# Two unused 96-byte tiles behind the right-hand weight pools of a fused linear-attention and two-MLP kernel

## The chip, the cores and the metric

The kernel runs on one core of one Trainium2 chip. The metric is the device time of one execution in microseconds (us): the median over several runs. The profile is one execution, taken by the hardware profiler; its span is the time from the first to the last instruction. Engines are named as in the profile: PE (TensorE matmul), PEld (TensorE weight load), DVE (VectorE), ACT (ScalarE), POOL (GpSimd), SP (SyncE, which issues most DMAs).

## The reference

Three stages follow each other, in float32.

```python
# 1. delta-rule linear attention: B=4, H=8, S=768, D=48
k_n = k / (norm(k) + 1e-6)
for t in range(S):
    y[t] = q[t] @ state
    v_old = state^T k_n[t]
    state = state + beta[t] * outer(k_n[t], v[t] - v_old)
# 2. squared-relu MLP on x = y as [3072 tokens, 384]
x = relu(x @ w_in) ** 2 @ w_out          # 384 -> 2048 -> 384
# 3. max-of-three MLP
h = maximum(maximum(x @ w1, x @ w2), x @ w3)   # 384 -> 768
out = h @ w_out2                                # 768 -> 384
```

## The kernel before

**Stages.** The 768 positions are cut into six steps of 128 positions; with four batches a step holds 512 tokens. Per step the attention runs in chunked form (`gram`, `solve`, `values`, `chain`: thousands of small float32 matmuls of 32 to 64 columns, long chains of small DVE operations in `solve`). `moe1` then does the first MLP for the 512 tokens of the step: 16 blocks of 128 hidden features, per block nine matmuls into one bank (`hidden`) and nine into three accumulating banks (`project`). After the last step comes the second MLP: `maxout` (27 matmuls per block of 128 features, six blocks) and `project2` (18 matmuls per 128 tokens). The small attention matmuls of later steps are interleaved with `moe1` of earlier ones; from about 515 us on no attention is left.

**Wide matmuls.** Every float32 operand of the two MLPs is kept as two float32r parts, high and low (names ending in h and l), and a product is made of three matmuls (`three`: high by high, high by low, low by high). One matmul has a stationary operand of 128x128, which PE loads first (a weight load, PEld), and a moving operand of 512 columns, which it streams. In `moe1` the stationary tiles are `wih`, `wil` (first weights) and `wo` (a ring of four, second weights), the moving ones are `xh`, `xl` and `gh`, `gl`. In `maxout` the stationary tiles are `b0h` to `b2l` and the moving ones `xh`, `xl` or `x2h`, `x2l`. In `project2` the stationary tiles are the hidden values `m0h`, `m0l` or, in turn by step, `m1h`, `m1l`, and the moving ones are the weights `b3h`, `b3l` with 384 columns.

**Order.** A planner in the kernel records all operations of stage one and two, and of stage three apart, and writes out a fixed order on each engine by its own costs and due times. Each engine then works through its order strictly. Every operation is issued by one helper, so all rows of the profile have line L330, and they are told apart by tile names.

**Places in memory.** Tiles lie in pools of SBUF. The left pools (`const`, the attention pool `apool`, later `bwp`) grow from low addresses, the right ones from the top of the memory downwards: `wpool` holds `wih`, `wil` and the four `wo`; after it is closed, `bsb` holds `m1h` and `m1l`. Within a partition all left tiles that wide matmuls read (`xh`, `xl`, `gh`, `gl`, `x2h`, `x2l`, all `b` tiles, `m0h`, `m0l`) start at byte 384 of a 512-byte block, since the tiles ahead of them come to such a sum and each of them is a multiple of 512 bytes. All tiles of the two right pools are multiples of 512 bytes too and start at byte 480 of a block, 96 bytes further. A stationary slice of 128 float32 values is 512 bytes long, a moving one 2048 (or 1536 in `project2`), so all slices keep the offset of their tile.

Of the kernel before, what the change touches and what calls it, by code (L numbers as in the profile page):

```python
# [10 lines left out]
F32 = mybir.dt.float32  # L11
# [324 lines left out]
def kernel(  # L336
# [31 lines left out]
    P = 128  # L368
# [29 lines left out]
    wpool = es_w.enter_context(tc.tile_pool(name="wpool", bufs=1, side="right"))  # L398
# [13 lines left out]
    def tiles(pool, n, shape, dtype, name):  # L412
        return [pool.tile(shape, dtype, tag=f"{name}{i}", name=f"{name}{i}") for i in range(n)]

    def one(pool, shape, dtype, name):
        return pool.tile(shape, dtype, tag=name, name=name)
# [20 lines left out]
    wih = one(wpool, [P, KD, DFF], F32R, "wih")  # L437
    wil = one(wpool, [P, KD, DFF], F32R, "wil")
    wo_ring = Ring(tiles(wpool, 4, [P, 2, DM], F32R, "wo"))

    kq = [one(apool, [P, 2, HP, 2, 64], F32, x) for x in ("kt", "qt")]
    kt, qt = ([x[:, i] for i in range(2)] for x in kq)
# [492 lines left out]
    with tc.manual_schedule():  # L935
# [71 lines left out]
        def load_x2(t):  # L1007
            raw, (hi, lo) = x2r[t % len(x2r)], x2()
            pl.sync.dma_start(out=raw, in_=x2d[t].rearrange("r p c -> p r c"))
            for r in range(KD):  # L1010
                pl.scalar.activation(hi[:, r], raw[:, r], AF.Copy)
                pl.vector.tensor_tensor(lo[:, r], raw[:, r], hi[:, r].bitcast(F32), op=sub)
            return hi, lo

        def maxout(f, x, m2):
            ph = []
            fs = slice(f * P, f * P + P)
            for i in range(3):
                ph.append(b_ring())
                for r in range(KD):  # L1020
                    with pl.together():
                        three(ph[i], bw[i, "h"][:, r, fs], bw[i, "l"][:, r, fs],
                              x[0][:, r], x[1][:, r], r == 0, r == KD - 1)
                    pl.at += 1
            m = r_ring()
            pl.scalar.activation(m, ph[0], AF.Copy)
            pl.vector.tensor_tensor(m, m, ph[1], op=ALU.max)
            pl.vector.tensor_tensor(m, m, ph[2], op=ALU.max)
            pl.scalar.activation(m2[0][:, f], m, AF.Copy)
            pl.vector.tensor_tensor(m2[1][:, f], m, m2[0][:, f].bitcast(F32), op=sub)  # L1030

        def project2(t, b, m2):
            po = o_ring()[:, 0:DM]
            bs = slice(b * P, b * P + P)
            for f in range(NF2):
                with pl.together():
                    three(po, m2[0][:, f, bs], m2[1][:, f, bs], bw[3, "h"][:, f],
                          bw[3, "l"][:, f], f == 0, f == NF2 - 1)
                pl.at += 0.75
            ob = ob_ring()  # L1040
            pl.scalar.activation(ob, po, AF.Copy)
            pl.sync.dma_start(out=ov[t, b], in_=ob)
# [9 lines left out]
        es_w.close()  # L1052
        bsb = ctx.enter_context(tc.tile_pool(name="bsb", bufs=1, side="right"))
        m_all.append([one(bsb, [P, NF2, TB], F32R, "m1" + x) for x in "hl"])
        for n, t in enumerate(order):
            if n + 1 < NS:
                x = x2() if order[n + 1] == NS - 1 else load_x2(order[n + 1])
                maxout(0, x, m_all[(n + 1) % 2])
            for b in range(B):
                project2(t, b, m_all[n % 2])  # L1060
            if n + 1 < NS:
                for f in range(1, NF2):
                    maxout(f, x, m_all[(n + 1) % 2])
# [31 lines left out]
```

## Time and profile before

| | |
|---|---|
| median of 3 runs | 951.26 us (950.89 to 952.01) |
| span of the profiled execution | 946.6 us |
| median less that span | 4.7 us |
| PE busy | 879.0 us, 93% of the span |
| PEld busy | 733.6 us, 77% |
| DVE busy | 588.9 us, 62% |
| ACT busy | 443.7 us, 47% |
| PE matmuls | 9388 |

The profile gives no time for the profiled execution other than its span, so the 4.7 us stand for what lies before the first and after the last instruction and for the difference between executions. Ends of matmuls are modelled: how close together matmuls run is read from the distance between their starts, not from their durations (a 512-column matmul shows some 390 to 406 ns and the next one starts long before that).

### The profile page before, as it was taken

The numbers are of one execution on the slowest core, as the hardware profiler recorded it, in microseconds if no ns is written. First come the engines' busy times: TensorE is split into PE (matmuls) and PEld (weight loads), VectorE is DVE, ScalarE is ACT, GpSimd is POOL, SyncE is SP. The second block draws the span as 40 slices with busy tenths as digits, with TensorE's granted clock in tenths as the row PEclk, the third lists the DMA queues.
The fourth block names the chain that finished last, engine by engine and source line by source line (L and its number), as shares of the span: only waits on it lengthen the run. The fifth ranks groups of instructions, "written<-read, shape, count | busy, mean of one in ns | idle before, by whom it ended". The sixth has DMA issues, their size and how long they took to land.

```text
span 946.6 us, 22413 instructions
## 1 busy us (share of the span) xinstructions
PE 879.0 (93%) x9388; PEld 733.6 (77%) x9388; DVE 588.9 (62%) x1256; ACT 443.7 (47%) x835; POOL 23.3 (2%) x33
## 2 busy tenths in 40 slices
PE   5536789999999989999999999999999999999998
PEld 4426778877777777877887888888898989898987
DVE  4999998899758957955953499893323232323221
ACT  6446468974465464565456567663222122121121
POOL 2001001000000010010000000000000000000000
PEclk9555799999999999999999999999999999999999
DMA  9744468777646646343422567670020100000000
GB/s 169 145 117 124 105 186 228 164 179 181 155 97 123 171 93 117 112 119 79 125 85 86 184 189 230 185 224 6 1 68 1 68 1 34 0 26 9 26 9 34
DMA packets 186276, 100.64 MB, mean 106 GB/s; under 512 B 150080, under 2 KB 166208, under 8 KB 186176
## 3 DMA queue, kind: packets, MB, share of 16 engines
q1 hardware_dynamic: 185328, 99.02, 40.3%
q8 instruction: 73, 1.20, 0.5%
q10 hardware_dynamic: 848, 0.20, 0.1%
q14 instruction: 27, 0.22, 0.1%
HBM read 79.53 MB, written 14.94 MB: 100 GB/s over the span
## 4 chain that ended last, share of the span: by engine, by line
PE 78%; DVE 14%; ACT 4%; issue 2%; DMA 1%; DVEq 0%; ACTq 0%
PE ps L330 78%; DVE xs L330 3%; DVE T L330 2%; DVE tmp L330 2%; DVE t L330 2%; ACT G L330 1%; DVE W L330 1%; DMA raw<-in_moe_w_in_dram 1%; DVE L L330 1%; ACT W L330 1%; ACT r L330 1%; DVE wil L330 1%; ACT US L330 1%; DVE gl L330 0%; DVE US L330 0%
## 5 line engine op out<-in xcount | busy, mean ns | idle before, releaser
L330 DVE TENSOR_TENSOR r<-r,ps 128x512 f32<-128x512 f32 x72 | 49.5, 688 | 178.7 <-PE ps L330 176.7
L330 PE MATMUL ps<-gh,wo 128*128 128x512 f32 (+1 forms) x624 | 159.5, 384 | 1.1 <-ACT gh L330 0.9
L330 ACT ACTIVATE r<-ps 128x512 f32<-128x512 f32 (+1 forms) x140 | 80.0, 572 | 165.3 <-PE ps L330 149.2
L330 PEld LDWEIGHTS ps<-gh,wo 128*128 128x128 f32 x624 | 111.6, 190 | 26.1 <-ACT gh L330 1.4
L330 PE MATMUL ps<-xh,wih 128*128 128x512 f32 (+1 forms) x312 | 123.1, 395 | 2.0 <-ACT r L330 1.7
L330 PE MATMUL ps<-xh,wil 128*128 128x512 f32 (+1 forms) x312 | 119.3, 382 | 0.9 <-issue 0.9
L330 PE MATMUL ps<-xl,wih 128*128 128x512 f32 (+1 forms) x312 | 119.0, 381 | 0.0
L330 DVE TENSOR_TENSOR gl<-r,gh 128x512 fp32r<-128x512 f32 (+1 forms) x104 | 67.1, 647 | 52.9 <-ACT gh L330 50.5
L330 PE MATMUL ps<-gl,wo 128*128 128x512 f32 (+1 forms) x312 | 85.9, 383 | 2.5 <-DVE gl L330 1.3
L330 PEld LDWEIGHTS ps<-xh,wih 128*128 128x128 f32 x312 | 59.7, 191 | 16.3 <-ACT r L330 3.5
L330 PEld LDWEIGHTS ps<-xh,wil 128*128 128x128 f32 x312 | 60.0, 192 | 12.3 <-issue 1.3
L330 PEld LDWEIGHTS ps<-xl,wih 128*128 128x128 f32 x312 | 59.8, 192 | 11.9
L330 PEld LDWEIGHTS ps<-gl,wo 128*128 128x128 f32 x312 | 56.4, 190 | 15.3 <-DVE gl L330 1.9
L330 ACT ACTIVATE gh<-r 128x512 fp32r<-128x512 f32 (+1 forms) x104 | 62.0, 596 | 10.0 <-PE ps L330 7.6
L330 ACT ACTIVATE G<-ps 32x256 f32<-32x256 f32 (+3 forms) x132 | 55.4, 432 | 22.5 <-PE ps L330 20.4
L330 DVE TENSOR_TENSOR T<-T,tmp 128x31 f32<-128x31 f32 (+15 forms) x186 | 63.0, 338 | 3.5
L330 DVE TENSOR_TENSOR tmp<-L,T 128x31 f32<-128x31 f32 (+15 forms) x186 | 62.8, 337 | 3.3
L330 ACT ACTIVATE r<-r 128x512 f32<-128x512 f32 (+1 forms) x104 | 62.0, 596 | 2.4
L330 PE MATMUL ps<-W 64*64 64x64 f32 x1536 | 47.0, 249 | 12.3 <-ACT W L330 9.7
L330 PEld LDWEIGHTS ps<-W 64*64 64x64 f32 x1536 | 40.2, 159 | 19.2 <-ACT W L330 12.2
L330 DVE TENSOR_SCALAR xs<-xs 128x384 f32<-128x384 f32 x112 | 40.6, 362 | 16.4 <-ACT xs L330 15.6
L330 ACT ACTIVATE m0h<-r 128x512 fp32r<-128x512 f32 x18 | 11.4, 632 | 67.2 <-DVE r L330 67.2
(149 smaller groups left out, 1663.0 us busy)
## 6 DMA issues: line engine op xcount, KB each, us to landing
wo<-wod SPq DMA_DIRECT2D x88, 384.0 KB, 3.4
raw<-in_moe_w_out_dram SPq DMA_DIRECT2D x22, 384.0 KB, 3.6
raw<-in_moe_w_dram SPq DMA_DIRECT2D x18, 384.0 KB, 3.9
raw<-in_moe_w_in_dram SPq DMA_DIRECT2D x16, 384.0 KB, 4.2
wod<-wo SPq DMA_DIRECT2D x16, 384.0 KB, 3.7
vn<-in_v_dram SPq DMA_DIRECT2D x24, 192.0 KB, 4.3
kn<-in_k_dram SPq DMA_DIRECT2D x24, 192.0 KB, 4.4
out_dram<-ob SPq DMA_DIRECT2D x24, 192.0 KB, 1.9
```

Source lines behind the costliest of these rows:

```text
L330: self.plan.add(self.name, lambda: fn(*args, **kw), cost, [out], ins, flow, late)
```

## The change

Two tiles that nothing writes or reads are allocated, one as the last tile of `wpool`, one as the last of `bsb`, each of 24 float32 values (96 bytes) per partition. As the right-hand pools end at the top of the memory, each pool starts 96 bytes lower: `wih`, `wil`, `wo` and `m1h`, `m1l` then start at byte 384 of a 512-byte block in place of 480. Nothing else has another address. The order of instructions is the same as before on all five engines, and so are the semaphores that each waits for.

```diff
@@ -437,6 +437,7 @@
     wih = one(wpool, [P, KD, DFF], F32R, "wih")
     wil = one(wpool, [P, KD, DFF], F32R, "wil")
     wo_ring = Ring(tiles(wpool, 4, [P, 2, DM], F32R, "wo"))
+    one(wpool, [P, 24], F32, "edge")
@@ -1052,6 +1053,7 @@
         es_w.close()
         bsb = ctx.enter_context(tc.tile_pool(name="bsb", bufs=1, side="right"))
         m_all.append([one(bsb, [P, NF2, TB], F32R, "m1" + x) for x in "hl"])
+        one(bsb, [P, 24], F32, "edge1")
```

## Rows read from the trace of the kernel before

**Rows 1.** Busy time of each engine in three stretches of the span.

```profile
core 0: us, PE busy (x) PEld busy (x) DVE busy (x) ACT busy (x) POOL busy (x), PEclk, DMA share, GB/s
0.00:226.00 226.00, 172.66 (x2839) 146.96 (x2840) 204.16 (x515) 137.54 (x293) 12.90 (x22) 0.83 0.65 159
226.00:435.00 209.00, 198.31 (x3376) 158.71 (x3374) 153.18 (x302) 115.09 (x205) 8.55 (x9) 1.00 0.54 123
435.00:645.00 210.00, 210.00 (x1766) 168.91 (x1767) 147.30 (x317) 126.17 (x227) 1.89 (x2) 1.00 0.52 155
```

**Rows 2.** Chain of work that ended last, its longest piece: start, us, what.

```profile
434.97 508.01 PE ps L330 x3072
```

**Rows 3.** Timeline of PE in the first MLP: start us, us, matmul.

```profile
599.69 0.40 PE L330 MATMUL ps<-xh,wil 128*128 128x512 f32 x1
...
602.97 0.40 PE L330 MATMUL ps<-xh,wih 128*128 128x512 f32 x1
```

**Rows 4.** Timeline of PE in maxout of the second MLP.

```profile
685.16 0.39 PE L330 MATMUL ps<-xl,b0h 128*128 128x512 f32 x1
...
690.15 0.33 PE L330 MATMUL ps<-b3h,m0h 128*128 128x384 f32 x1
```

**Rows 5.** Busy time by engine, first MLP, with much and little beside it.

```profile
550.00:640.00 90.00, 90.00 (x386) 72.34 (x385) 79.11 (x169) 61.92 (x114) 0.00 (x0) 1.00 0.67 209
...
640.00:644.50 4.50, 4.50 (x21) 3.62 (x20) 0.69 (x1) 2.14 (x4) 0.00 (x0) 1.00 0.02 4
```

**Rows 6.** Timeline of PE at the seam of the two MLPs.

```profile
646.29 0.39 PE L330 MATMUL ps<-x2l,b0h 128*128 128x512 f32 x1
...
647.20 0.62 PE L330 MATMUL ps<-gh,wo 128*128 128x512 f32 x2
...
653.43 0.39 PE L330 MATMUL ps<-x2h,b1h 128*128 128x512 f32 x1
...
655.47 0.39 PE L330 MATMUL ps<-x2h,b0h 128*128 128x512 f32 x1
```

**Rows 7.** Timeline of PE where maxout follows project2.

```profile
702.65 0.39 PE L330 MATMUL ps<-xh,b0h 128*128 128x512 f32 x1
...
704.74 0.39 PE L330 MATMUL ps<-xh,b1h 128*128 128x512 f32 x1
```

**Rows 8.** Busy time by engine in project2, first with m1, then with m0.

```profile
740.00:751.00 11.00, 11.00 (x65) 11.00 (x64) 1.00 (x2) 2.10 (x4) 0.00 (x0) 1.00 0.15 54
...
789.00:800.00 11.00, 11.00 (x65) 11.00 (x65) 1.25 (x2) 2.11 (x4) 0.00 (x0) 1.00 0.13 47
```

**Rows 9.** Groups of PE, 226 to 435 us: count, busy us, mean ns.

```profile
L330 PE MATMUL ps<-gh,wo 128*128 128x512 f32 x202 | 55.5, 401 | 0.0
L330 PE MATMUL ps<-xh,wih 128*128 128x512 f32 x96 | 39.5, 411 | 0.4 <-ACT r L330 0.4
```

**Rows 10.** Groups of PE by form, 435 to 653 us.

```profile
L330 PE MATMUL ps<-gh,wo 128*128 128x512 f32 x276 | 73.6, 398 | 0.0
L330 PE MATMUL ps<-xh,wih 128*128 128x512 f32 x132 | 53.0, 402 | 0.0
```

**Rows 11.** Timeline of PE: matmuls of 256 columns; later, small ones in a row.

```profile
153.12 0.87 PE L330 MATMUL ps<-gh,wo 128*128 128x256 f32 x6
...
155.94 0.51 PE L330 MATMUL ps<-gl,wo 128*128 128x256 f32 x3
...
176.81 1.16 PE L330 MATMUL ps<-W 64*64 64x64 f32 x64
```

**Rows 12.** Groups by form: DVE's writes of low weight parts, right and left.

```profile
L330 DVE TENSOR_TENSOR wil<-xs,wih 128x384 fp32r<-128x384 f32 x16 | 8.8, 552 | 2.9 <-ACT wih L330 2.8
...
L330 DVE TENSOR_TENSOR b1l<-xs,b1h 128x384 fp32r<-128x384 f32 x6 | 3.3, 557 | 0.8 <-ACT b1h L330 0.6
```

**Rows 13.** DMA issues into a right-hand tile: count, size, us to landing.

```profile
wo<-wod SPq DMA_DIRECT2D x88, 384.0 KB, 3.4
```

## The prediction

> **What bounds the kernel now.** I read the busy time by stretches first. Up to 226 us DVE works 204 of 226 us and PE waits for it; from 226 to 435 us PE works 198.3 of 209 us; from 435 us on it has no idle time at all (210.00 of 210), at a granted clock of 1.00, which is the 2.4 GHz level [rows 1]. The chain that ended last says the same: its last 508 us are PE alone, 3072 matmuls without a break [rows 2]. So from 435 us to the end each nanosecond between two matmuls counts in full, before 226 us hardly any does, and in between it is mixed.
>
> Then the pace of the wide matmuls, by their starts in the timeline, where no attention is left. In the first MLP 14 matmuls of 512 columns take 602.97 - 599.69 = 3.28 us, 234.3 ns each [rows 3]. In the second MLP 22 matmuls of the same size take 690.15 - 685.16 = 4.99 us, 226.8 ns each [rows 4]. At 2.4 GHz 512 columns are 213.3 ns, so the one kind has 21 ns on top and the other 13.5. Both have the same shapes, moving tiles from the left pools (`xh` and `xl` in both) and a new weight load for each matmul. What differs: the stationary tile of the first lies in the right pool, 96 bytes off the moving tile within 512, that of the second in the left pool, at the same offset.
>
> Other differences have to be ruled out. The first MLP has DVE, ACT and DMAs beside it, the second little. But with DVE busy 79 of 90 us and DMA at 0.67 the 90 us hold 386 matmuls (two of them cut by the edges: 234.4 ns each), and in 4.5 us with DMA at 0.02, hardly any DVE and the same tiles there are 21 (again two cut: 234 to 237 ns) [rows 5]. The activity beside it doesn't set the pace. At the seam the two kinds stand mixed within 10 us: the last four of a left-hand group take 0.91 us, 228 ns each; then 27 matmuls, of which 9 are right-hand ones in groups of two or three, take 6.23 us, 231 ns each, left-hand ones among them too; then nine left-hand ones 2.04 us, 226.7 ns each [rows 6]. A right-hand load disturbs, and those behind it need some matmuls to find back.
>
> **The change, part by part.**
>
> *First pool (`wih`, `wil`, `wo`).* Nothing is added to any engine and nothing is moved in any order; the wide matmuls of the first MLP get the offsets of those in the second. If the offset is what differs, each gains 234.3 - 226.8 = 7.5 ns.
>
> From 435 us to the end of the first MLP there are 276 with `gh` and `wo`, half as many, 138, with `gl`, and three times 132 with `wih` and `wil` [rows 10], 810 in all: 810 x 7.5 = 6.1 us. Not each runs at the best pace at once: behind `project2`, where the width changes, the first nine left-hand matmuls take 2.09 us, 232.2 ns each, 49 ns more in all than nine at 226.8 [rows 7]. Each cluster of small attention matmuls will cost such a restart. Between 435 and 645 us there are 1766 matmuls less some 780 wide ones [rows 1, 10], about 985 small ones; a cluster is some 64 of them [rows 11], so about 15 restarts, 0.75 us. That leaves 5.3 us, on the path in full (PE never waits there).
>
> From 226 to 435 us there are 202 + 101 + 3 x 96 = 591 [rows 9], 4.4 us. Some 2785 small matmuls [rows 1] make about 44 restarts, 2.2 us. Of the 2.2 us left I take half, 1.1 us: PE idles 10.7 us of this stretch, and where it waits for a result of ACT or DVE, a faster PE only waits longer. The bounds are 0 and 4.4.
>
> Before 226 us I take nothing: what hides it is DVE's 204 of 226 us [rows 1]. The 256-column matmuls stand there, 24 of them in 155.94 - 153.12 = 2.82 us, 117.5 ns each [rows 11], 10.8 over their columns. With the 13.5 of the left-hand ones they would be slower, by 2.7 ns; there are 288 (the first `HALF` = 8 blocks of the first step, done in two halves of the tokens: 2 x 8 x 18), 0.8 us at most if the cover were gone.
>
> *Second pool (`m1h`, `m1l`).* I take nothing. Here the trace has both cases side by side: 11 us of `project2` hold 65 matmuls of 384 columns with the right-hand `m1` and 65 with the left-hand `m0` [rows 8]. This row is also the best argument against the whole theory, since the same 96 bytes do no harm there; the offset then must matter for 512 columns and not for 384. As the weights in rows 3 and 4 differ by place alone, and clearly, I keep to it, but not with certainty.
>
> *Others that touch the tiles.* DVE writes a low part of 384 columns in 552 ns to the right and 557 to the left [rows 12]: nothing. The DMAs into `wo` land after 3.4 us [rows 13] and no stretch from 435 us on shows PE idle for them; even some tenths more would be hidden by the ring of four.
>
> *Sum.* 5.3 + 1.1 = 6.4 us: a span of 946.6 - 6.4 = 940.2 us, and from the median 951.26 (4.7 us above that span) 944.9 us. Its own range: without any restart loss and with all of the middle stretch 6.1 + 4.4 = 10.5 us, 940.8; with twice the restart loss and nothing from the middle 6.1 - 1.5 = 4.6 us, 946.7. What is late next: nothing from 435 us on, since ACT has 126 and DVE 147 busy of 210 us there; at a pace 3% faster DVE goes from 79 to about 82 of each 90 us in its fullest part [rows 5].
>
> **The rivals.**
>
> *Nothing changes (951.3 us).* The offset isn't the cause, but something that goes with the right pool or with the first MLP, such as the distance in memory or the change between two kinds of moving tile; then the change moves addresses and no time. For it: rows 8, equal for both pools. Against it: the seam [rows 6], where the pace follows the stationary tile, and the best pace survives the change of `x2h`, `x2l` and of the `b` tiles.
> The Trainium skill speaks for this rival: "TensorE: Matmul & The Clock Gate", section "Step-by-step: what each phase is for", says that PE has two independent read ports to SBUF, and that loading the next weights takes no read bandwidth from the running matmul. By that rule no placement matters and the time stays. The trace agrees in rows 8 and not in rows 3 against rows 4.
>
> *A small part only (949.0 us).* The good pace is reached but not kept: the first MLP goes between two kinds of moving tile and two of weights every nine matmuls, and if each such change is a restart, all run at the 232.2 ns of rows 7, 2.1 ns better than now: 810 x 2.1 = 1.7 us and half of 591 x 2.1 = 0.6, together 2.3 us. For it: the second MLP never shows such alternation. Against it: there the changes of tile go by unseen.
>
> *Slower (959.6 us).* Two reads at one offset meet each other and hinder each other more than two 96 bytes apart, in the first MLP, where a load follows each matmul. The price, for want of a row, is the same difference with its sign turned: 7.5 ns x (810 + half of 591) = 8.3 us. It decides from 1.7 ns per wide matmul on (1.9 us over 1105). Against it: the left-hand tiles have equal offsets and run best.
>
> **How the numbers follow.** My forecast 0.71, the small part 0.11, nothing 0.12, slower 0.06. About 0.2%, 1.9 us, is what a measurement of this kernel can tell from no change; forecast and small part lie beyond it, so faster is 0.82, same 0.12, slower 0.06. The predicted time is the forecast's, 944.9 us. The range takes in its own bounds and the small part, 940.8 to 949.0, and leaves out 0.18.
>
> **What would show it.** In the profile after, the starts in the first MLP without attention should lie 227 ns apart in place of 234.3, and a window of 90 us there should hold some 397 matmuls in place of 386; the second MLP should be unchanged, `project2` at 65 in 11 us for both; the first MLP's last matmul should come 5 to 7 us earlier, with PE still without idle time from 435 us on; the stretch before 226 us should keep its length. The prediction is wrong if the pace stays at 234 (the pool or the stage, not the offset), settles at about 232 (restarts), or rises. It is wrong in its size if the middle stretch gives all or none, which PE's idle time between 226 and 435 us would show.

## The result and the profile after

The changed kernel takes 942.44 us (median of 6 runs, 939.6 to 943.68) against 951.24 us before (6 runs): ratio 0.9904, 95% interval 0.9887 to 0.9921, so 7.5 to 10.7 us faster. The profiled execution has a span of 940.6 us, 6.0 us less than before, and took 943.03 us as a whole, one of the longer of the six. The six executions of the changed kernel take 2.1 to 3.1 us more than their spans; by that the kernel before, with a span of 946.6 us, took about 949 us when it was profiled (an estimate), less than each of its six timed runs (950.53 to 953.11). So the two profiles show less of the gain than the medians do.

Busy time of each engine after, in the stretches of [rows 1]:

```profile
0.00:226.00 226.00, 169.53 (x2836) 144.27 (x2837) 204.20 (x513) 137.50 (x293) 12.90 (x22) 0.83 0.65 158
226.00:435.00 209.00, 196.88 (x3394) 159.72 (x3396) 153.30 (x304) 114.97 (x205) 8.56 (x9) 0.99 0.55 124
435.00:645.00 210.00, 210.00 (x1788) 173.04 (x1781) 147.46 (x319) 126.46 (x228) 1.90 (x2) 1.00 0.51 155
```

The first two stretches look much as before (2836 and 3394 matmuls against 2839 and 3376), DVE still fills the first one, and PE still never idles in the third, but holds 22 matmuls more there. The end of the chain that ended last, after (start, us, what), shows the same by time:

```profile
434.14 0.56 issue
434.70 502.30 PE ps L330 x3071
937.07 0.49 ACT ob L330
```

The long piece of PE begins at the same place as before, 434.70 against 434.97 us, and takes 502.30 us in place of 508.01 [rows 2]. So 5.7 of the 6.0 us come behind 435 us and 0.3 us ahead of it.

The timeline of PE after, first MLP, at the place of [rows 3], then the seam of the two MLPs, at the place of [rows 6]:

```profile
599.33 0.39 PE L330 MATMUL ps<-xh,wil 128*128 128x512 f32 x1
...
600.46 1.52 PE L330 MATMUL ps<-gh,wo 128*128 128x512 f32 x6
601.82 0.84 PE L330 MATMUL ps<-gl,wo 128*128 128x512 f32 x3
602.50 0.39 PE L330 MATMUL ps<-xh,wih 128*128 128x512 f32 x1
```

```profile
641.26 0.62 PE L330 MATMUL ps<-gh,wo 128*128 128x512 f32 x2
...
645.34 0.39 PE L330 MATMUL ps<-x2h,b2h 128*128 128x512 f32 x1
```

From 599.33 to 602.50 us there are 14 matmuls in 3.17 us, 226.4 ns each, where there were 234.3. At the seam 18 matmuls that go between right-hand and left-hand weights seven times take 4.08 us, 226.7 ns each: the disturbance is gone, and a change of tile is no restart. Ninety microseconds of the first MLP, and 11 us each of `project2`, first with `m1`, then with `m0`, answer to [rows 5] and [rows 8]:

```profile
550.00:640.00 90.00, 90.00 (x399) 74.53 (x398) 77.97 (x167) 61.56 (x114) 0.00 (x0) 1.00 0.64 202
735.00:746.00 11.00, 11.00 (x65) 11.00 (x64) 0.65 (x1) 1.48 (x3) 0.00 (x0) 1.00 0.16 56
784.00:795.00 11.00, 11.00 (x66) 11.00 (x65) 0.69 (x1) 1.66 (x4) 0.00 (x0) 1.00 0.15 54
```

399 matmuls in place of 386, and `project2` as it was.

### The profile page after: what moved, and what is told of

Same layout as the page of the kernel before. It is cut to its first block, busy times and chain, and to the rows that moved or that the text cites. A ratio compares the mean times of both kernels' runs of the same rounds, so it can differ in the third digit from the quotient of the medians.

```text
span 940.6 us, 22413 instructions
## 1 busy us (share of the span) xinstructions
PE 868.4 (92%) x9388; PEld 731.2 (78%) x9388; DVE 588.4 (63%) x1256; ACT 443.1 (47%) x835; POOL 23.4 (2%) x33
## 4 chain that ended last, share of the span: by engine, by line
PE 74%; DVE 14%; ACT 5%; DMA 3%; issue 3%; SPq 0%; DVEq 0%; ACTq 0%
PE ps L330 74%; DVE xs L330 3%; DVE T L330 2%; DVE tmp L330 2%; ACT G L330 2%; DVE t L330 2%; DVE W L330 1%; DMA raw<-in_moe_w_out_dram 1%; DMA raw<-in_moe_w_in_dram 1%; ACT r L330 1%; ACT W L330 1%; DVE gl L330 1%; ACT US L330 1%; DVE L L330 1%; ACT xs L330 0%
## 5 line engine op out<-in xcount | busy, mean ns | idle before, releaser
L330 PE MATMUL ps<-gh,wo 128*128 128x512 f32 (+1 forms) x624 | 156.3, 379 | 2.8 <-ACT gh L330 2.0
```

Source lines behind the costliest of these rows:

```text
L330: self.plan.add(self.name, lambda: fn(*args, **kw), cost, [out], ins, flow, late)
```

## The experiments

"Distance" below is the start of the stationary tile less that of the moving tile, within 512 bytes: 96 before, 0 in the changed kernel, in the first MLP. The left pools could be shifted too, by a tile ahead of `ident` or as the first of `bwp`. A pace is the mean time between the starts of neighbouring wide matmuls, from the 20th of an unbroken row of them on, read from the trace of each kernel (steps of over 300 ns, where PE waited, are left out). All distances tried are multiples of 32 bytes.

**One pool at a time.**

```diff
     # e1_first_pool
+    one(wpool, [P, 24], F32, "edge")
     # e2_second_pool
+        one(bsb, [P, 24], F32, "edge1")
```

> Only the tile behind the first pool (wih, wil, wo); m1 stays 96 bytes off. If the whole gain comes from the 512-column matmuls of the first MLP, this kernel does all that the change does: about 942 us, first MLP at 227 ns per wide matmul, 6 us less span from 435 us on. If m1 has a share, it lies between 942 and 951 us, and project2 with m1 shows it.

> Only the tile behind the second pool (m1h, m1l); the first pool stays 96 bytes off. If the offset matters for 512 columns and not for the 384 of project2: no change, 951 us, first MLP at 234 ns. If m1 has a share: below 950 us, and project2 with m1 would have more than 65 matmuls in 11 us.

The first pool alone gives 940.68 us against 950.09 on that chip, ratio 0.9908 (0.9884 to 0.9932), with the first MLP at 227 ns. The second alone gives 949.21 us, ratio 0.9995 (0.9979 to 1.0012), with the first MLP at 234 ns. The last pieces of their chains, e1 and then e2, where the kernel before has 508.01 us [rows 2]:

```profile
433.99 502.27 PE ps L330 x3072
```

```profile
434.39 508.10 PE ps L330 x3072
```

The whole effect is that of `wih`, `wil` and `wo`; the second unused tile does nothing that these runs can tell.

**Equal distance or good alignment.**

```diff
     # e3_left_moved
+    one(const, [P, 24], F32, "edge0")
     ident = one(const, [P, P], F32, "ident")
     # e4_right_at_128
+    one(wpool, [P, 88], F32, "edge")
+        one(bsb, [P, 88], F32, "edge1")
```

> All left tiles move 96 bytes up to offset 480, the right ones stay at 480: offsets are equal again, but no tile lies on a 64-byte boundary. Theory 'equal offset of stationary and moving tile': both MLPs at 227 ns per wide matmul, about 942 us. Theory 'alignment' (a tile at 480 is badly placed, one at 384 well): both MLPs at 234 ns, some 7 us more in the second MLP than before, about 958 us.

> Right tiles moved 352 bytes down, to offset 128: on a 128-byte boundary, but 256 bytes from the left ones within 512. Theory 'alignment': 227 ns per wide matmul, about 942 us. Theory 'equal offset': the first MLP is not at 227 ns; if any difference disturbs alike, 234 ns and 951 us; project2 with m1, 256 bytes off now, shows whether 384 columns stay free of it at that distance as well.

Windows of the first MLP, of e3 and then of e4 (80 us long; the kernel with a distance of -96, below, has 344 there):

```profile
550.00:630.00 80.00, 80.00 (x355) 66.24 (x354) 73.55 (x159) 56.43 (x105) 0.00 (x0) 1.00 0.67 208
```

```profile
550.00:630.00 80.00, 80.00 (x355) 66.24 (x354) 72.94 (x158) 55.70 (x104) 0.00 (x0) 1.00 0.68 208
```

Both have the good pace. e3, with every tile off the 64-byte boundaries, still runs both MLPs at 227 ns: alignment is not the cause. But e4 runs at 227 ns as well with a distance of 256, and 941.7 us, ratio 0.992 (0.9895 to 0.9945), is as good as the changed kernel: equal offsets are not needed. Each theory lost one of the two tests. e3 as a whole gained less, 944.04 us, ratio 0.9948 (0.9929 to 0.9966); its last piece of PE is as short (502.32 us) but begins at 436.91 us, so what it loses lies ahead of that, and why was not found.

**A table of distances.** Six kernels, each with a tile in `wpool`, which sets the distance of the first MLP, and one at the start of `bwp`, which sets that of `maxout` with `xh` (with `x2h` it stays 0).

```diff
     # e5, e6, e7, e8: n = 8, 120, 16, 48 and m = 8, 40, 48, 24;  e11, e12: n = 72, 56 and m = 56, 72
+    one(wpool, [P, n], F32, "edge")
         bwp = ctx.enter_context(tc.tile_pool(name="bwp", bufs=1))
+        one(bwp, [P, m], F32, "edge2")
```

> Right tiles 64 bytes past the left ones (offset 448), and the second MLP's left tiles 32 bytes past xh and xl, so that maxout with xh has a distance of 32 and with x2h one of 0. 'Any multiple of 64 is good': first MLP 227 ns, maxout with xh 234 ns. 'Any multiple of 128' or 'of 256': both 234 ns. 'Only a short way past the moving tile is bad': both 234 ns. Maxout with x2h 227 ns by all.

> Right tiles 128 bytes past the left ones (offset 0), the second MLP's left tiles 160 past xh. 'Multiple of 64' and 'of 128': first MLP 227 ns, maxout with xh 234 ns. 'Multiple of 256': both 234 ns. 'Only a short way past is bad' (32 to 96 bytes): both 227 ns.

> Right tiles 32 bytes past the left ones (offset 416), the second MLP's left tiles 192 past xh. 'Multiple of 64': first MLP 234 ns, maxout with xh 227 ns. 'Multiple of 128' or '256': both 234 ns. 'Only a short way past is bad': first MLP 234 ns, maxout with xh 227 ns.

> Right tiles 96 bytes short of the left ones (offset 288), the second MLP's left tiles 96 past xh: the distance of the kernel before, now within the left pool and in the second MLP. If the distance is the cause, maxout with xh runs at 234 ns (486 matmuls, 3.6 us more in the second MLP) and with x2h at 227; if pool or stage is, at 227 both. First MLP: 'multiple of 64, 128 or 256' 234 ns, 'only a short way past is bad' 227 ns.

e8 answers whether pool or stage has a part: `maxout` of the second MLP, all tiles left, in the timeline of PE, first with `x2h` (distance 0), then with `xh` (distance 96):

```profile
656.16 0.39 PE L330 MATMUL ps<-x2h,b0h 128*128 128x512 f32 x1
...
660.92 0.39 PE L330 MATMUL ps<-x2h,b2h 128*128 128x512 f32 x1
```

```profile
700.87 0.39 PE L330 MATMUL ps<-xh,b1h 128*128 128x512 f32 x1
...
705.79 0.39 PE L330 MATMUL ps<-xh,b0h 128*128 128x512 f32 x1
```

Each pair of rows spans 21 matmuls: 4.76 us, 226.7 ns each, and 4.92 us, 234.3 ns each. That is to the tenth the pace of the first MLP before. The same weights, in the same pool and stage, lose 7.6 ns per matmul by a distance of 96 alone; that it isn't `xh` itself, the kernel before shows, where the same tiles at a distance of 0 take 226.8 ns [rows 4]. The window of its first MLP (distance -96, that is 416):

```profile
550.00:630.00 80.00, 80.00 (x344) 64.35 (x344) 71.74 (x154) 54.45 (x101) 0.00 (x0) 1.00 0.64 203
```

As 32, 64, 128, 160, 192 and 416 all disturb, neither a multiple of 64 or 128 nor "a short way past" fits; 256 was the only multiple left that did. The last two kernels of this kind looked for a still better place:

> Right tiles 320 bytes past the left ones, the second MLP's left tiles 224 past xh. 'Only multiples of 256 hold the best pace': both 229 to 234 ns. 'The disturbance shrinks towards 256' (192 gave 228.9): 224 at 227 to 229, 320 alike.

> Right tiles 384 bytes past the left ones, the second MLP's left tiles 288 past xh. 'Only multiples of 256': both 229 to 234 ns. 'Shrinks towards 256, grows beyond': 288 near 227 to 229, 384 near 233. A pace below 226.7 at any distance would make a kernel faster than the changed one.

The paces found, in ns, 512 columns (with the kernel that gave each), and the same for `project2` with 384 columns, whose distance is that of `m1` and `b3`:

```
distance   512 columns                           384 columns (project2, m1)
  0        226.7  after, e1, e3                  173.3  after, e3, e8
 32        233.3  e5 (maxout), e7
 64        233.3  e5                             175.4  e5
 96        234.3  before; e8 (maxout)            173.3  before, e1
128        232.6  e6
160        233.3  e6 (maxout)
192        228.9  e7 (maxout)
224        233.3  e11 (maxout)
256        226.8  e4                             173.3  e4
288        233.3  e12 (maxout)
320        233.3  e11                            175.4  e12
384        232.5  e12                            176.1  e11
416        233.4  e8                             176.7  e7
448                                              173.3  e6
```

Of the distances tried, only 0 and 256 keep the best pace for 512 columns, and the four pairs that lie 256 apart (32 and 288, 64 and 320, 128 and 384, 160 and 416) agree within 0.1 ns: as far as these pairs show, what counts is the distance within 256 bytes. No distance tried is better than 226.7 ns, so no kernel here beats the changed one. The idea that the disturbance shrinks towards 256 fell: 192 is mild, 224 is not. Single times of these six kernels (946.5 to 952.0 us against 947 to 948 of the kernel before beside them) tell little, since they have gains and losses in both MLPs.

**The same two kernels again.** No edit; for the stretch before 435 us, and for the time.

> The kernel before once more, for a second profile: how much do its stretches differ between executions? Theory 'the gain is the pace after 435 us alone, 6 us, and the rest of the measured difference is a lucky pair of medians': 196 to 197 us for the stretch from the 2900th to the 6300th matmul, as in the first profile. Theory 'the stretch before 435 us varies by microseconds from execution to execution': another length by 1 us or more.

> The changed kernel once more, timed in five rounds: a ratio of 0.990 to 0.992 as measured, and in the profile again 226.7 ns per wide matmul and 6 us less from 435 us to the end of the first MLP. Whether the stretch before 435 us gains anything shows against the other profiles: forecast 1.1 us, the first pair of profiles showed none.

e10 repeats the gain: 939.05 us against 947.97, ratio 0.9914 (0.9888 to 0.9939). The ends of their chains, e9 and then e10:

```profile
432.07 508.00 PE ps L330 x3072
```

```profile
429.15 502.51 PE ps L330 x3072
```

In this pair the last piece is 5.5 us shorter, and it begins 2.9 us earlier: together the 8.4 us between the two spans (943.7 and 935.3 us). In the first pair it began only 0.3 us earlier. So the stretch before 435 us does vary by microseconds from one execution to the next: the kernel before itself reached that piece at 434.97 and at 432.07 us. The place where they part is seen in the timeline of PE from 350 to 359.5 us. The kernel before in its first profile, then in its second (e9), the changed one in its first, then in its second (e10); the bracket is PE's idle time ahead of the row:

```profile
354.92 0.27 PE L330 MATMUL ps<-W,US 128*48 128x64 f32 x2 [1.55 <-issue]
358.93 0.33 PE L330 MATMUL ps<-W 64*64 64x64 f32 x5 [0.84 <-issue]
```

```profile
357.18 0.34 PE L330 MATMUL ps<-W 64*64 64x64 f32 x5 [0.83 <-issue]
```

```profile
353.76 0.27 PE L330 MATMUL ps<-W,US 128*48 128x64 f32 x2 [1.24 <-issue]
358.86 0.48 PE L330 MATMUL ps<-W 64*64 64x64 f32 x5 [1.93 <-issue]
```

```profile
355.34 0.34 PE L330 MATMUL ps<-W 64*64 64x64 f32 x5 [0.56 <-issue]
```

Both first profiles have a gap in the midst of a row of equal small matmuls that both second ones don't have, and the changed kernel's first has a longer second gap behind it. The profile names nothing that ends them ("issue"), but the DMA records of the traces show what they go with. One queue carries instructions alone:

```profile
q8 instruction: 73, 1.20, 0.5%
```

These are 73 transfers of 16 KB in the first profile of the kernel before, one for about each 128 of its 9388 matmuls. All fourteen kept profiles together have 101 gaps of PE of over 0.5 us between 226 and 440 us that are put down to "issue". All stand at one of ten places in PE's order, some 128 matmuls or a multiple of that apart, and each ends 1.2 to 1.9 us (median 1.4) behind the end of such a transfer, though the transfers begin 3 to 24 us apart. The two gaps of the kernel before end 1.46 and 1.40 us behind one. So PE very probably waits there for its own instructions; no run here changed their loading, and why they come in time in one execution and not in another stays open. The faster pace doesn't make the first of the two gaps rarer: it stands in four of the five profiles with the good pace in the first MLP (after, e1, e3, e4) and in two of the nine others (before, e5).

## Why the prediction was right

The direction, the mechanism and the main place were right: 942.4 us lies in the range of 940.8 to 949.0, 2.5 us under the 944.9 forecast. The size was less good: the forecast sum of 6.4 us lies below the measured 7.5 to 10.7. By its steps:

*The pace.* Forecast 226.8 ns, found 226.4 to 226.7, and shown to come from the distance alone: by e1 and e2 (which pool), by e8 (the same slow pace in another pool and stage) and by e3 (not the alignment).
On this, the section "Step-by-step: what each phase is for" of "TensorE: Matmul & The Clock Gate" in the Trainium skill says that the load of the next weights takes no read bandwidth from the running matmul. The trace doesn't agree as far as time goes: 234.3 against 226.7 ns by placement alone, so the measurement decides. What happens between the two reads inside the chip, no run here shows.

*From 435 us on.* Forecast 6.1 less 0.75 for restarts, 5.3 us; measured 5.7 and 5.5 us. The restarts are there, but the term was more than twice too large. In the timeline of PE after, behind a cluster of 64 small matmuls:

```profile
449.72 0.39 PE L330 MATMUL ps<-xh,wil 128*128 128x512 f32 x1
...
450.88 1.53 PE L330 MATMUL ps<-gh,wo 128*128 128x512 f32 x6
452.24 0.84 PE L330 MATMUL ps<-gl,wo 128*128 128x512 f32 x3
```

The first five take 1.16 us, 232 ns each, the next six 1.36 us, 226.7 ns each. Added up from 435 us on, that is 0.29 us in each of the changed kernel's two profiles, for 12 and 11 clusters: some 25 ns a cluster, where the forecast took 49 for each of 15 from [rows 7].

*From 226 to 435 us, and before.* Forecast 1.1 us and nothing, within 0 and 4.4; measured 0.3 and 2.9 us for both stretches together in two pairs of profiles. This is the term that was mis-sized: behind 435 us the change gives 5.5 to 5.7 us in each pair, so the medians (8.8, 8.9 in the repeat) leave some 3 us for what lies ahead, within the bounds but well above 1.1. One reason can be counted: the stretch has 28 clusters in the trace before, not 44, and at 25 ns each they cost 0.7 us and not 2.2 (an estimate from the sum above), so the wide matmuls there could give 3.7 us. How much of it arrives depends on PE's waits.

The profiles don't show that gain steadily. In the ten profiles in which PE then runs to the end in one piece, that piece begins at 429.15, 433.99, 434.70 and 436.91 us with the good pace (e10, e1, after, e3), and at 431.64 to 434.97 us with the pace of before (before, e2, e6 to e9). Of those without the first gap, e10 begins 2.5 us ahead of the earliest other; of those with it, after and e1 begin 0.3 and 1.0 us ahead of the kernel before and e3 1.9 us behind it. Both executions of the second pair were quick for their kernel: e9's, 945.83 us, was quicker than the eleven other runs of the kernel before beside it (946.18 to 951.66), and e10's, 937.41, was the quickest of its six. So the medians gain some 3 us more than the part behind 435 us gives; how these come about ahead of 435 us is not shown.

*The second pool.* Forecast nothing, found nothing (e2).

*The reading of rows 8.* They were the best argument against the theory, met by "the offset matters for 512 columns and not for 384". That answer was wrong: at distances of 64, 320, 384 and 416 `project2` is disturbed too (175.4 to 176.7 ns in place of 173.3), and 96, the one distance that the kernel before shows, happens to be free of it.

*The theory itself* was too narrow: not the same offset within 512 is needed, but a distance of nothing within 256 (e4).

*The rivals.* "Nothing changes" and "slower" fell by the pace. "A small part only" fell by the seam, where the pace holds through changes of tile.

## What to carry to other kernels

Where PE runs back to back with a weight load for each matmul, compare the distance between the starts of neighbouring matmuls by tile, not their durations: a few nanoseconds that go with a tile and not with the load of the other engines point to its place in memory. Then shift a pool by an unused tile until stationary and moving tiles of float32r lie a multiple of 256 bytes apart; it cost nothing here but 96 bytes, and the wide matmuls of the whole stage gained. Where other waits stand between such a gain and the end, measure more than one profile before saying what it gave.

## What the runs showed that was not expected

The distance between the tile that PE loads and the one that it streams counts within 256 bytes as far as the table goes, for 512 columns of float32r by up to 7.6 ns in 227, at 32 bytes as much as at 128 (233.3 and 232.6 ns), and differently for 384 columns: 96 costs nothing there and 416 costs 3.4 ns.

In the changed kernel's first profile the gap of 1.93 us at 357 us is followed by matmuls that start about twice as far apart: a granted clock of 0.50, the lower level of 1.2 GHz, over 2 us, and of 0.79 over the 3 us behind them, so the lower level for a part of these too. Busy time around it:

```profile
352.00:359.00 7.00, 3.83 (x149) 3.06 (x145) 3.67 (x5) 2.15 (x5) 0.00 (x0) 0.99 0.51 92
359.00:361.00 2.00, 2.00 (x12) 1.13 (x13) 0.14 (x1) 1.40 (x4) 0.00 (x0) 0.50 0.28 65
361.00:364.00 3.00, 3.00 (x67) 2.84 (x67) 2.94 (x5) 2.88 (x6) 0.00 (x0) 0.79 0.29 60
```

PE was busy 3.83 of the 7 us ahead of it. So in that execution the gaps cost more than their length, which may be part of why it was one of the slower ones.
